# Reading back the inverse transforms of the first 512 tokens: a scratch of their own for the last group's rows, a later place in TensorE's list, and scratch rows of 2 KB

## The chip, the core and the metric

The kernel runs on one core of a Trainium2 chip. The core has a TensorE for matrix products (PE, with weight loads listed apart as PEld), VectorE (DVE), ScalarE (ACT), GpSimd (POOL), and SyncE (SP), which issues most DMA transfers. Each engine works through a list of its own; a semaphore holds an instruction until what it reads is there. The engines have on-chip memory (SBUF) of 128 partitions, and TensorE writes its sums to PSUM. DRAM is reached by DMA alone. DMA issues stand in the lists of SP, ScalarE and GpSimd, so what an issuing engine waits for holds up its transfers, and an issue takes its turn among that engine's other work.

The metric is the device time in microseconds (us) of one execution; lower is better.

## The reference

One layer on 2048 tokens of width 640: a normalization with modulation, a long convolution by a state-space model, a second normalization, and a gated feed-forward stage of width 1728.

```python
K = jnp.einsum("dn,dnl,dn->dl", Cc, P, dB).real          # P = exp(dt*A*l), the convolution kernel
Kf = rfft2(pad(K)); Uf = rfft2(pad(up))
y = irfft2(Uf * Kf, s=(1, 2 * L))[..., :L] + u * Dskip
...
x = A_u
sa, ca, ga, sb, cb, gb = ...                             # from silu(c) @ w_mod
h = _layernorm(x) * (1 + ca) + sa
x = x + ga * conv(h)
h = _layernorm(x) * (1 + cb) + sb
x = x + gb * (silu(h @ w1) * (h @ w3)) @ w2
```

## The kernel before

**Stages.** The convolution of length 2048 is a Fourier transform in two steps, 32 (NA) by 64 (NB) points, as matrix products. The 640 channels are NDC = 5 chunks of 128 (DC). A front part normalizes and transforms the input; a loop over 40 steps, whose order of work is the hand-written list `ROUND`, makes the transform of the convolution kernel and runs the steps of the chunks; its last eight steps' worth of chunk work, the eight groups g = 0 to 7 of the last chunk, stand in a plain loop over `tk` behind it. Then follows the feed-forward stage, on 512 tokens (four tiles of 128) at a time.

**A group.** For each chunk, eight groups of four frequencies go through: `stage2` (the second step of both forward transforms: products of uk with the table s2, in PSUM as p; 8 products), `k_copy` (ScalarE copies half of p to kc), `products` and `sums` (VectorE: T, then Y), and `inverse1` (8 products of Y with the table i1 into pz). s2 and i1 come by SP, in three buffers each. `z_store` copies pz (to zt, or in the last chunk to a tile of the pool h) and stores it in the DRAM scratch zs. For chunks 0 to 3 SP stores every second group (512 KB); for the last chunk `z_last` stores each group (256 KB) from ScalarE's queue.

**The second inverse step** needs, for a tile of 128 tokens, the rows of all 32 frequencies and both parts (64 rows) of 4 positions, so it reads zs across. The table for it is i2. A tile of such rows has the tag A in the profile, as the tiles of the exponentials before it had. In zs before, these rows lie as [chunk, position, part, frequency, channel], and a tile's load takes 4 pieces of 512 bytes for each of its 64 rows.

**The first 512 tokens** (tiles 0 to 3, `early`). The feed-forward stage begins with them, so their inverse is made beside the last groups. `x_part` takes chunks 0 to 3 from A (8 products, py) and VectorE adds the input xe into xm; `x_stats` are the statistics of the four chunks (st). ScalarE copies the fifth part of xe. The last chunk is taken apart. Groups 6 and 7 (from NG = 6) take the near way: `near_rows` makes their 16 rows straight from Y (8 products into a part of pz, and a copy to h), `near_cols` spreads them to the 512 tokens (pl<-h), with weights that `near_tables` makes on GpSimd; nothing goes through DRAM. Groups 0 to 5 take the far way: `z_last` stores them in zs, reads 24 frequencies of both parts back into the third part of A (two loads for each tile, those of tiles 0 to 2 on SP behind group 5's store, those of tile 3 on ScalarE behind group 6's), and `far_cols` adds 4 products for each tile (pl<-A; 64 rows, of which the unused ones are set to zero by memsets). VectorE then adds pl into xm, completes the statistics (mv), GpSimd and VectorE make the scales rs, `x_first` normalizes tiles 0 and 2 on ScalarE and 1 and 3 on VectorE (also called T in the profile), TensorE transposes them (ps<-ident,T) and `turn_a` makes xA, the operand of the feed-forward stage. Fillers (fill<-ident, ps<-idle) are products without use that keep TensorE's clock up.

**First weights.** `plain` computes the feed-forward blocks with weights split in a high and a low part (gh and gl for w1, uh and ul for w3): ScalarE casts the loaded rw, VectorE subtracts. Those of the first block, f = 0, are loaded behind the last i1 on SP.

**What sets the order.** A scheduler lists the instructions of each engine; `keep`, `ordered`, `acopy` and `keep_in_program_order` pin them to the order of the source, and `issue_after` puts a transfer behind a given instruction. In the loop over `tk`, i is the group whose `iv` and `zt` were just issued; this is where the work on the first 512 tokens is placed:

```python
if i == 3:
    x_stats(0)
if i in (2, 3, 5):
    x_part((0, 0, 0, 1, 0, 2)[i])
if i == 4:
    x_stats(1)
if i == 6:
    x_stats(2)
    near_cols(6)
```

`x_part(3)` stands in `near_rows` of group 7. In the trace, rows of py, pl and the near pz share L735, the line of the helper `ordered`; L148 is the helper of ScalarE's copies, and L111 that of `InOrder`, through which the feed-forward stage issues. The trace counts each of these fp32 products twice (x16 where the program has 8).

## Time and profile before

| | |
|---|---|
| runs (us) | 931.51, 931.76, 939.97; median 931.76 |
| the profiled execution (us) | 929.92 |
| its span in the profile (us) | 928.1 |
| granted TensorE clock, mean | 0.996 |
| busy: PE, PEld, DVE, ACT, POOL (us) | 890.6, 695.1, 698.6, 548.5, 259.1 |
| moved by DMA | 140.68 MB |

The busy time is a sum over the whole span and says little of a stage. The stretches of the span that the prediction shows give busy time, clock and transfers of a few microseconds each; the chain of waits goes back from the last instruction, at each step to what released it; the timelines give one engine's instructions in order, and in brackets how long the engine was idle before, and what ended it. "ACTq" and "SPq" are DMA issues on ScalarE's and SP's lists. Time in a timeline starts at the start of the span. A DMA group's last number is the median from issue to landing.

### The profile page before, as it was taken

To read this page: it belongs to the slowest core of one execution; us is meant where nothing else is said; L and a number is where in the kernel's file an instruction comes from. 1 tells how busy PE (TensorE), PEld (TensorE's weight loads), DVE (VectorE), ACT (ScalarE), POOL (GpSimd) and SP (SyncE) were. 2 spreads that over 40 slices of the span, in tenths; PEclk is the share of its full clock that TensorE was granted. 3 is DMA by queue.
4 is the path that set the end of the run, shared out by engine and by line. 5 is a ranking of instruction groups with operands and counts; after the bars stand their busy time and mean duration, and the time that the engine had idled before them with its cause. 6 is when DMAs were issued, how large, how long until landed. Compare 5 with 4: busy or idle time off the path is not lost.

```text
span 928.1 us, 21045 instructions
## 1 busy us (share of the span) xinstructions
PE 890.6 (96%) x8461; PEld 695.1 (75%) x8461; DVE 698.6 (75%) x1254; ACT 548.5 (59%) x811; POOL 259.1 (28%) x274
## 2 busy tenths in 40 slices
PE   5999889999999998999999999999999999999998
PEld 3766567777777666778888887778888888888886
DVE  6699888999999966877666655686876666664665
ACT  4899899999999742573433333566633333333432
POOL 3633454445446320231222201210522222200000
PEclk9999999999999999999999999999999999999999
DMA  8755897655656886942122117974222211103452
GB/s 257 238 207 201 265 230 216 177 160 156 177 160 173 205 258 217 249 180 86 57 85 85 46 49 211 260 257 154 89 71 72 85 58 57 58 28 100 146 179 101
DMA packets 103765, 140.68 MB, mean 152 GB/s; under 512 B 20212, under 2 KB 62964, under 8 KB 103668
## 3 DMA queue, kind: packets, MB, share of 16 engines
q1 hardware_dynamic: 100108, 129.48, 46.8%
q0 software_dynamic: 2048, 7.34, 2.4%
q10 hardware_dynamic: 1512, 2.52, 0.8%
q8 instruction: 66, 1.08, 0.5%
q14 instruction: 31, 0.25, 0.1%
HBM read 107.85 MB, written 31.46 MB: 150 GB/s over the span
## 4 chain that ended last, share of the span: by engine, by line
PE 69%; ACT 13%; DVE 11%; DMA 4%; issue 2%; SPq 0%; ACTq 0%; DVEq 0%; POOLq 0%; POOL 0%
PE ps L111 58%; PE p L676 3%; ACT A L145 2%; ACT ph L145 2%; DVE E L597 2%; PE pz L727 2%; ACT cs L145 2%; DVE uk L111 2%; PE pm L111 2%; ACT L145 2%; DVE A L604 1%; PE pt L637 1%; ACT kc L148 1%; DMA A<-zs 1%; DMA s<-in_s_dram 1%
## 5 line engine op out<-in xcount | busy, mean ns | idle before, releaser
L111 DVE TENSOR_TENSOR s<-ps,s 128x512 f32<-128x512 f32 x138 | 95.0, 689 | 79.9 <-PE ps L111 79.6
L111 DVE TENSOR_TENSOR gl<-rw,gh 128x640 fp32r<-128x640 f32 x87 | 77.9, 895 | 64.2 <-ACT gh L111 64.1
L570 POOL TENSOR_TENSOR ph<-thi,iota 128x1024 int32<-128x1024 int32 x40 | 85.9, 2149 | 141.9 <-DVE A L608 94.9
L111 ACT CAST gh<-rw 128x640 fp32r<-128x640 f32 x87 | 63.3, 727 | 102.8 <-PE ps L111 66.4
L111 POOL TENSOR_TENSOR S<-rw 128x256 f32<-128x256 f32 x46 | 35.4, 771 | 192.2 <-DVE S0l L111 167.9
L111 PE MATMUL ps<-xA,gh 128*128 128x512 f32 x280 | 88.4, 393 | 0.1
L111 PE MATMUL ps<-gh,uh 128*128 128x512 f32 x224 | 87.4, 390 | 0.0
L111 PE MATMUL ps<-gl,uh 128*128 128x512 f32 x224 | 87.2, 389 | 0.0
L676 PE MATMUL p<-uk,s 128*64 128x256 f32 x640 | 77.9, 385 | 7.2 <-DVE Y L701 2.4
L111 PE MATMUL ps<-gh,ul 128*128 128x512 f32 x208 | 81.1, 390 | 0.0
L676 PEld LDWEIGHTS p<-uk,s 128*64 128x64 f32 x640 | 44.6, 136 | 29.9 <-DVE Y L701 3.5
L111 PEld LDWEIGHTS ps<-xA,gh 128*128 128x128 f32 x280 | 52.2, 188 | 13.6 <-issue 1.0
L111 PE MATMUL ps<-xA,gl 128*128 128x512 f32 x140 | 54.5, 390 | 0.0
L604 DVE TENSOR_TENSOR A<-A,ph 128x1024 f32<-128x1024 f32 x40 | 51.9, 1297 | 0.0
L111 ACT ACTIVATE s<-ps 128x512 f32<-128x512 f32 (+1 forms) x33 | 19.6, 595 | 53.1 <-PE ps L111 53.1
L597 DVE TENSOR_TENSOR E<-A,cs 128x1024 f32<-128x1024 f32 x40 | 50.2, 1256 | 0.6 <-ACT A L145 0.6
L111 PEld LDWEIGHTS ps<-gl,uh 128*128 128x128 f32 x224 | 42.1, 188 | 9.0
L111 PEld LDWEIGHTS ps<-gh,uh 128*128 128x128 f32 x224 | 42.0, 188 | 8.8
L727 PE MATMUL pz<-Y,i 64*128 64x128 f32 x640 | 45.3, 282 | 0.7 <-ACT h L148 0.4
L111 PEld LDWEIGHTS ps<-gh,ul 128*128 128x128 f32 x208 | 39.0, 188 | 8.3
L574 POOL TENSOR_TENSOR ph<-ph,phi 128x512 int32<-128x512 int32 x40 | 44.5, 1114 | 2.5
L727 PEld LDWEIGHTS pz<-Y,i 64*128 64x128 f32 x640 | 39.7, 191 | 7.2 <-issue 5.9
(251 smaller groups left out, 2287.7 us busy)
## 6 DMA issues: line engine op xcount, KB each, us to landing
rw<-in_w_dram SPq DMA_DIRECT2D x52, 320.0 KB, 3.0
us<-u SPq DMA_DIRECT2D x16, 640.0 KB, 3.2
s<-in_s_dram SPq DMA_DIRECT2D x40, 256.0 KB, 5.1
i<-in_i_dram SPq DMA_DIRECT2D x40, 256.0 KB, 3.3
rw<-in_wg_dram SPq DMA_DIRECT2D x31, 320.0 KB, 3.3
rw<-in_wu_dram SPq DMA_DIRECT2D x28, 320.0 KB, 2.9
uk<-us SPq DMA_DIRECT2D x32, 256.0 KB, 4.6
zs<-zt SPq DMA_DIRECT2D x16, 512.0 KB, 4.5
```

The source lines that it names most:

```text
L111: ins = fn(*args, **kw)
L145: return tc.keep_in_program_order(S.activation(*args, **kw))
L148: return tc.keep_in_program_order(S.copy(out, in_))
L570: keep(G.tensor_tensor(p, bc(thi[:, s * SD:s * SD + SD], 2, NPH), bc(iota, 1, SD), op=OP.mult))
L574: keep(G.tensor_tensor(p[:, :, :NA], p[:, :, :NA], bc(phi[:, s * SD:s * SD + SD], 2, NA), op=OP.add))
L597: keep(V.tensor_tensor(EC[s][:, :, 1:3, :], AA[s][:, :, 1:3, :], mid(cs[s]), op=OP.mult))
L604: keep(V.tensor_tensor(A[:, :, 1:3, :], A[:, :, 1:3, :], mid(ph[s]), op=OP.mult))
L637: keep(PE.matmul(pt[c * 64:c * 64 + 64, g, :], kk[:, g, :], s1[:, c, :], start=True, stop=True, tile_position=(0, c * 64)))
L676: keep(PE.matmul(p2[par * 64:par * 64 + 64, pi, c, :], s2[:, pi * 2 + par, c * 64:c * 64 + 64], uk[:, 0:kn + 1:kn, f, :], start=True, stop ...
L727: ins = keep(PE.matmul(pz[:, par, (g % 2) * 2 + pi, :], i1[r, pi, c, :], Y[r, pi, c, :], start=(c == 0), stop=(c == 1), tile_position=(par ...
```

## The change

**Scratch layout.** zs becomes [chunk, frequency, part, position, channel]; a tile's load is then 64 rows of 2 KB, and a store writes 512 bytes at a time. The rows of i1, i2 and of the tiles A follow. **Last group.** Group 5's rows for the four tiles (positions 0 to 15) are also stored by two transfers of ScalarE in the new scratch ze, ahead of the group's whole store. SP loads the rows of groups 0 to 4 (40) for each tile from zs behind group 4's store, and the 8 rows of group 5 from ze behind the stores of group 5; ScalarE loads nothing. `far_cols` uses 48 rows, and the memsets are gone. **Later inverses.** `x_part` of tiles 0, 1, 2 stands at i = 4, 5, 6. **First weights.** Their loads stand ahead of the last i1 on SP. ScalarE's casts (`first_high`, into tiles of the pool rw) stand at i = 6 and in `near_rows` of group 7, VectorE's subtractions (`first_low`, in two parts, into tiles of the pool h) at the end of i = 6 and behind `x_first`. **Smaller.** The near rows take their part of i1 from the table i2d, which grows from 80 to 336 columns; two kinds of VectorE's instructions in `x_first` are pinned.

```diff
-    i2 = np.concatenate([np.cos(ang).T, -np.sin(ang).T] * 2)
+    i2 = np.concatenate([np.stack([np.cos(ang).T, -np.sin(ang).T], axis=1).reshape(2 * NA, NA)] * 2)
...
-    i1 = i1.reshape(*i1.shape[:-1], 2, NB).swapaxes(-1, -2).reshape(i1.shape)
+    i1d = i1[:, -4:].reshape(P, 4, 2, 2, NB)[..., :16].swapaxes(-1, -2)
...
-                i2d[fl, :, c, i * NA:i * NA + NA] = i2[c * NA + (6 + i) * 4 + fl]
+                i2d[fl, :, c, i * NA:i * NA + NA] = i2[2 * ((6 + i) * 4 + fl) + c]
             i2d[fl, :, c, 2 * NA:] = np.eye(16)
-    i2d = i2d.reshape(P, 2 * NA + 16)
+    i2d = np.concatenate([i2d.reshape(P, 2 * NA + 16), i1d.reshape(P, 8 * NA)], axis=1)
...
-    zs = dram.tile([NDC, NB, 2, NA, DC], F32, name="zs")
+    zs = dram.tile([NDC, NA, 2, NB, DC], F32, name="zs")
+    ze = dram.tile([4, 2, 16, DC], F32, name="ze")
...
-            near_rows(g, i1, Y, pz[:, 0, 2 - 2 * (g % 2), :])
+            near_rows(g, Y, pz[:, 0, 2 - 2 * (g % 2), :])
...
-    near = {}
...
+    near, first_w = {}, []
+
+    def first_high(i):
+        if i == 0:
+            near["raw"] = [xp.tile([P, KD, P], F32, name="rw", bufs=5) for _ in range(2)]
+            for w, name in zip(near["raw"], ("wg", "wu")):
+                with tc.issue_after(i1_last[0].ins):
+                    w_get(w, 0, name)
+            near["lo4"] = h_tile(F32R)
+        hi = xp.tile([P, KD, P], F32R, name="rw", bufs=5)
+        acopy(hi, near["raw"][i])
+        lo = h_tile(F32R).rearrange("p (k c) -> p k c", k=4)
+        first_w.append((near["raw"][i], hi, lo, near["lo4"][:, i * P:i * P + P]))
+
+    def first_low(w, hi, lo, lo4):
+        for out, k in ((lo, slice(4)), (lo4, 4)):
+            tc.keep_in_program_order(V.tensor_tensor(out, w[:, k], hi[:, k].bitcast(F32), op=OP.subtract))
 
...
 
     def near_tables():
 
-        hc = h_tile()[:, :2 * NA + 16]
...
+            G.tensor_tensor(w.rearrange("p (b a) -> p b a", b=16), bc(hc[:, 2 * NA:2 * NA + 16], 2, NA),
                             bc(hc[:, i * NA:i * NA + NA], 1, 16), op=OP.mult)
         near["z"] = h_tile()
-        for x, z, st in early:
...
             for c in range(2):
                 for par in range(2):
                     r, fl = slice(par * 64, par * 64 + 64), pi * 2 + par
...
             x_part(3)
+            first_high(1)
             near_cols(7)
             far_cols()
...
+    far = slice(64, 64 + 8 * NG)
+
     def far_cols():
...
-                ordered(near["pl"][b * NA:b * NA + NA, j * P:j * P + P], i2[64:], z[64:, b, 2 * DC:], start=False, stop=True,
+                ordered(near["pl"][b * NA:b * NA + NA, j * P:j * P + P], i2[far], z[far, 2, b], start=False, stop=True,
...
-    zst = [zs[k].rearrange("b c f d -> (b c) f d") for k in range(NDC)]
-    zsv = zs.rearrange("k b c f d -> (c f) b k d")
+    zst = [zs[k].rearrange("f c b d -> (c b) f d") for k in range(NDC)]
+    zev = ze.rearrange("f c b d -> (f c) b d")
+    zsv = zs.rearrange("k f c b d -> k (f c) b d")
...
+        for c in range(2) if g == NG - 1 else ():
+            S.dma_start(ze[:, c].rearrange("f b d -> b f d"), zt[c * 64:c * 64 + 16])
         stored = S.dma_start(zst[NDC - 1][:, g * 4:g * 4 + 4], zt)
-        for j in (range(3), (3,), ())[g - NG + 1] if g >= NG - 1 else ():
+        for j in range(4) if NG - 2 <= g < NG else ():
+            r = slice(0, 8 * g + 8) if g < NG - 1 else slice(8 * g, 8 * g + 8)
             with tc.issue_after(stored.ins):
-                for c in range(2):
-                    r = slice(c * 32, c * 32 + 4 * NG)
-                    ins = (S if j == 3 else nc.sync).dma_start(
-                        early[j][1][64 + r.start:64 + r.stop, :, 2 * DC:], zsv[r, 4 * j:4 * j + 4, NDC - 1])
-                    if j < 3:
-                        zlast[0] = ins
-
+                zlast[0] = nc.sync.dma_start(early[j][1][64 + r.start:64 + r.stop, 2],
+                                             (zsv[NDC - 1, r] if g < NG - 1 else zev)[:, 4 * j:4 * j + 4])
...
-            q.dma_start(z[hh * 64:hh * 64 + 64, :, kk * DC:kk * DC + DC], zsv[:, 4 * j:4 * j + 4, k])
+            q.dma_start(z[hh * 64:hh * 64 + 64, kk], zsv[k, :, 4 * j:4 * j + 4])
...
+    def h_tile(dt=F32):
+        return xp.tile([P, 512], dt, name="h", bufs=18)
 
...
-        return z.rearrange("p k s b -> p (k s b)").rearrange("p (b d) -> p b d", b=4)
-
-    ZW = (2 * DC, 3 * DC)
+        return z.rearrange("p k s b -> p (k s b)").rearrange("p (k b d) -> p k b d", k=3, b=4)
+
+    ZK = (2, 3)
...
-                ordered(py[hh][c, :2 * DC], i2[r], z[r, b, :2 * DC], start=True, stop=True,
...
+                ordered(py[hh][c, :2 * DC], i2[r], z[r, :2, b], start=True, stop=True,
...
-            if i == 3:
-                x_stats(0)
-            if i in (2, 3, 5):
-                x_part((0, 0, 0, 1, 0, 2)[i])
-            if i == 4:
-                x_stats(1)
+            if i in (4, 5, 6):
+                x_part(i - 4)
+            if i in (5, 6):
+                x_stats(i - 5)
             if i == 6:
+                near_cols(6)
+                first_high(0)
                 x_stats(2)
-                near_cols(6)
+                first_low(*first_w[0])
...
-    for name in first_w:
-        first_w[name] = xp.tile([P, KD, P], F32, name="rw", bufs=5)
-        with tc.issue_after(i1_last[0].ins):
-            w_get(first_w[name], 0, name)
-
...
-            V.scalar_tensor_tensor(rs[:, 2, :], mv[:, 2 * pair:2 * pair + 2, 0], -1.0, rs[:, 1, :],
-                                   op0=OP.mult, op1=OP.mult)
+            tc.keep_in_program_order(V.scalar_tensor_tensor(rs[:, 2, :], mv[:, 2 * pair:2 * pair + 2, 0], -1.0, rs[:, 1, :],
+                                                            op0=OP.mult, op1=OP.mult))
...
-                    V.tensor_scalar(xn, x, mv[:, j, 0:1], rs[:, 1, i:i + 1], op0=OP.subtract, op1=OP.mult)
+                    tc.keep_in_program_order(V.tensor_scalar(xn, x, mv[:, j, 0:1], rs[:, 1, i:i + 1],
+                                                             op0=OP.subtract, op1=OP.mult))
...
-                n = ZW[hh]
-                PE.matmul(py[hh][c, :n], i2[r], z[r, b, :n], start=True, stop=True, tile_position=(r.start, c.start))
+                n = ZK[hh] * DC
+                PE.matmul(py[hh][c, :n], i2[r], z[r, :ZK[hh], b], start=True, stop=True, tile_position=(r.start, c.start))
...
-    ahead = {(0, n): w for n, w in first_w.items()}
+    ahead = {}
...
+        if isinstance(w[0], list):
+            return w[0][k], w[1][k]
...
-        ws = first_plain.pop() if first_plain else plain_weights(simple[0], last_sum)
+        ws = first_plain.pop() if first_plain else [
+            ([hi[:, k] for k in range(KD)], [lo[:, k] for k in range(4)] + [lo4]) for _, hi, lo, lo4 in first_w]
...
             x_first(tiles, mv4)
+            first_low(*first_w[1])
```

On TensorE, around groups 2 to 6 of the last chunk (pz<-Y is `inverse1`, or with 32x128 `near_rows`; p is `stage2`; py is `x_part`), the list before:

```order
L727 MATMUL pz<-Y,i_5029 128x128 x8
L735 MATMUL py<-A,i_64 32x256 x8
L676 MATMUL p_5064<-uk,s_5062 64x256 x8
L727 MATMUL pz<-Y,i_5075 128x128 x8
L735 MATMUL py<-A,i_64 32x256 x8
L676 MATMUL p_5113<-uk,s_5111 64x256 x8
L727 MATMUL pz<-Y,i_5124 128x128 x8
L676 MATMUL p_5150<-uk,s_5148 64x256 x8
L727 MATMUL pz<-Y,i_5161 128x128 x8
L735 MATMUL py<-A,i_64 32x256 x8
L676 MATMUL p_5201<-uk,s_5199 64x256 x8
L735 MATMUL pz<-Y,i_5212 32x128 x8
```

and now:

```order
L728 MATMUL pz<-Y,i_5026 128x128 x8
L677 MATMUL p_5048<-uk,s_5046 64x256 x8
L728 MATMUL pz<-Y,i_5059 128x128 x8
L677 MATMUL p_5080<-uk,s_5078 64x256 x8
L728 MATMUL pz<-Y,i_5091 128x128 x8
L752 MATMUL py<-A,i_65 32x256 x8
L677 MATMUL p_5130<-uk,s_5128 64x256 x8
L728 MATMUL pz<-Y,i_5141 128x128 x8
L752 MATMUL py<-A,i_65 32x256 x8
L677 MATMUL p_5185<-uk,s_5183 64x256 x8
L752 MATMUL pz<-Y,h 32x128 x8
L728 MATMUL pz<-Y,i_5196 128x128 x8
```

The inverses of tiles 0 and 1 (py) have each moved behind two further pairs of p and pz, and that of tile 2 from ahead of the last p to behind the next pz.

On ScalarE, from the copy of group 6's pz (h<-pz 128x2x2x128) to the normalization (T), the list before:

```order
L148 COPY h<-pz 128x2x2x128
L798 DMA zs<-h 128x512
L803 DMA A<-zs 24x4x128 x2
L148 COPY h<-pz 128x128
L148 COPY xm<-xe_3784 128x128
L148 COPY h<-pz 128x2x2x128
L111 CAST gh<-rw 128x640
L798 DMA zs<-h 128x512
L111 CAST uh<-rw 128x640
L111 ACTIVATE T_5371<-xm,rs_5364 128x640
L111 ACTIVATE T_5376<-xm,rs_5367 128x640
```

and now (the casts into rw are those of the first weights):

```order
L149 COPY h<-pz 128x2x2x128
L820 DMA zs<-h 128x4x128
L149 COPY xm<-xe_3557 128x128
L149 CAST rw<-rw 128x640
L149 COPY h<-pz 128x128
L149 COPY xm<-xe_3785 128x128
L149 CAST rw<-rw 128x640
L149 COPY h<-pz 128x2x2x128
L111 ACTIVATE T_5371<-xm,rs_5364 128x640
L820 DMA zs<-h 128x4x128
L111 ACTIVATE T_5376<-xm,rs_5367 128x640
```

The two loads of A and the two casts no longer stand between the copies of group 7 and the first T, and the last store has moved behind that T.

On SP, from the i1 tables of the last groups to the first loads of the feed-forward stage, before:

```order
L711 DMA i_5212<-in_i_dram 128x512
L711 DMA i_5252<-in_i_dram 128x512
L830 DMA rw<-in_wg_dram 128x640
L830 DMA rw<-in_wu_dram 128x640
L803 DMA A<-zs 24x4x128 x6
L1089 DMA xm<-in_x_dram 128x640 x2
L111 DMA A<-zs 64x4x128 x8
```

and now:

```order
L712 DMA i_5196<-in_i_dram 128x512
L848 DMA rw<-in_wg_dram 128x640
L848 DMA rw<-in_wu_dram 128x640
L712 DMA i_5261<-in_i_dram 128x512
L824 DMA A<-zs 40x512 x4
L824 DMA A<-ze 8x512 x4
L1101 DMA xm<-in_x_dram 128x640 x2
L111 DMA A<-zs 64x512 x8
```

The weights have moved ahead of the last i1, and six loads of 24 rows in pieces of 512 bytes have become four of 40 and four of 8 rows of 2 KB, the latter from ze.

More of the change, by code (lines that the diff above doesn't have):

```diff
@@ L737, in near_tables @@
     def near_tables():
-        hc = h_tile()[:, :2 * NA + 16]
+        hc = h_tile()[:, :2 * NA + 16 + 8 * NA]
+        near["i1"] = hc[:, 2 * NA + 16:].rearrange("p (g c b) -> p g c b", g=4, c=2)
         nc.sync.dma_start(hc, a["i2d"])
@@ L742, in near_tables, with near_rows @@
             w = near["w", NG + i] = h_tile()
[L743 removed]
+            G.tensor_tensor(w.rearrange("p (b a) -> p b a", b=16), bc(hc[:, 2 * NA:2 * NA + 16], 2, NA),
                             bc(hc[:, i * NA:i * NA + NA], 1, 16), op=OP.mult)
         near["z"] = h_tile()
[L746 to L749 removed]
+    def near_rows(g, Y, pd):
         for pi in range(2):
@@ L754, in near_rows @@
                     r, fl = slice(par * 64, par * 64 + 64), pi * 2 + par
-                    ordered(pd[fl * 32:fl * 32 + 32], i1[r, pi, c, :32], Y[r, pi, c, :],
+                    ordered(pd[fl * 32:fl * 32 + 32], near["i1"][r, (g - NG) * 2 + pi, c], Y[r, pi, c, :],
                             start=(c == 0), stop=(c == 1), tile_position=(par * 64, fl * 32))
@@ L813, in z_load @@
             kk = k - 2 * hh
-            q.dma_start(z[hh * 64:hh * 64 + 64, :, kk * DC:kk * DC + DC], zsv[:, 4 * j:4 * j + 4, k])
+            q.dma_start(z[hh * 64:hh * 64 + 64, kk], zsv[k, :, 4 * j:4 * j + 4])
     def x_tile():
         return xp.tile([P, D], F32, name="xm", bufs=6)
-    def h_tile():
-        return xp.tile([P, 512], F32, name="h", bufs=18)
+    def h_tile(dt=F32):
+        return xp.tile([P, 512], dt, name="h", bufs=18)
     def z_tile():
         z = tz.tile([P, SD, 3, NA], F32, name="A")
-        return z.rearrange("p k s b -> p (k s b)").rearrange("p (b d) -> p b d", b=4)
-    ZW = (2 * DC, 3 * DC)
+        return z.rearrange("p k s b -> p (k s b)").rearrange("p (k b d) -> p k b d", k=3, b=4)
+    ZK = (2, 3)
     def w_get(w, f, name, q=nc.sync):
@@ L1011, in tile_kernel @@
     xp = None
-    first_w = dict.fromkeys(("wg", "wu"))
     ROUND = (
@@ L1134, in z_place @@
         return wq.tile([P, 2, 2, 512], F32, name=both).rearrange("p a b c -> p (a b c)")[:, :4 * 3 * DC].rearrange(
-            "p (b d) -> p b d", b=4)
+            "p (k b d) -> p k b d", k=3, b=4)
     def x_place(name):
@@ L1323, in plain @@
                         for i in range(1 if lo else 2):
-                            end = PE.matmul(ps, ws[i][:, k, :], x[k][lo], start=(k + i + lo == 0),
+                            end = PE.matmul(ps, wk(ws, k)[i], x[k][lo], start=(k + i + lo == 0),
                                             stop=(lo == 1 and k == KD - 1))
```

8 lines of the change are left out of this document (3 added, 5 removed).

## The prediction

> **What bounds the kernel now.** I read the page first, then busy time by stretches, the chain of waits, and last the timeline of each engine around the place that the change touches.
>
> ```profile
> span 928.1 us, 21045 instructions
> ...
> 345.00:351.00 6.00, 4.81 (x62) 2.97 (x62) 3.78 (x11) 1.96 (x4) 0.18 (x1) 1.00 0.90 281
> ...
> 367.00:368.00 1.00, 0.00 (x0) 0.00 (x0) 0.00 (x0) 0.00 (x0) 0.00 (x0) 0.90 0.80 260
> ...
> 374.00:375.00 1.00, 1.00 (x5) 0.83 (x4) 1.00 (x2) 0.82 (x2) 0.00 (x0) 0.68 0.54 169
> ...
> 400.00:450.00 50.00, 49.82 (x230) 40.99 (x229) 35.27 (x56) 25.99 (x47) 11.81 (x15) 1.00 0.32 106
> ```
>
> A row of stretches gives its length, then the busy time of TensorE (PE), of its weight loads, of VectorE (DVE), ScalarE (ACT) and GpSimd, the granted clock, and the DMA engines' share and GB/s. TensorE fills the feed-forward stage (49.82 of 50 us), so whatever brings its first product forward shortens the whole run by as much. Two gaps stand ahead of it: 1.2 us of idle PE in 345 to 351, and one that holds all of 367 to 368. In the second the clock falls (0.90 there, a mean over a stretch that ends at 0.50), and in 374 to 375 (0.68) it comes back. The chain of waits (start, length, what) goes through both:
>
> ```profile
> 342.72 4.93 DMA A<-zs
> ...
> 364.25 4.27 DMA A<-zs
> ...
> 369.30 2.01 PE pz L727 x16
> 371.31 1.58 PE fill L735 x6
> ...
> 376.62 2.12 ACT xA L111 x3
> ```
>
> The rows of the last chunk that tile 3 of the first 512 tokens needs land at 368.5; then come the last inverse product (pz), fillers, seven idle products and the transposes (both ps), and at 376.62 copies into the first operand xA of the feed-forward stage. All that the change can win lies in these 31 us.
>
> **The change, part by part.**
>
> *Inverses of the first tiles later (`x_part`, tag py).*
>
> ```profile
> 345.89 0.62 PE L735 MATMUL py<-A,i 64*32 64x256 f32 x2
> 347.70 0.66 PE L735 MATMUL py<-A,i 64*32 64x256 f32 x14 [1.19 <-DMA A<-zs]
> 348.29 1.95 PE L676 MATMUL p<-uk,s 128*64 128x256 f32 x16
> 350.16 1.16 PE L727 MATMUL pz<-Y,i 64*128 64x128 f32 x16
> 351.25 0.66 PE L735 MATMUL py<-A,i 64*32 64x256 f32 x16
> ```
>
> Two of sixteen py products issue at 345.89, the other fourteen at 347.70, when the load of 342.72 has landed. Sixteen take 348.29 - 347.70 = 0.59, so two take 0.08 and the wait is 347.70 - 345.97 = 1.7 us. In the new order two stages of p (1.87) and pz (1.09) come before them: TensorE gets there at 345.89 + 2 x 2.96 = 351.8, 4.2 us after today's landing. The wait goes: **-1.7**. No instruction is added; the py products of tiles 1 and 2 also move behind pz, which costs nothing in sum. On VectorE their sums move behind the products of the next group; what this does to its end is worked out below.
>
> *The far rows (`z_last`, `far_cols`).* Before, groups 0 to 5 are read back after group 5's store has landed, tile by tile, and tile 3 from ScalarE's queue behind group 6's store.
>
> ```profile
> 357.79 0.66 PE L735 MATMUL py<-A,i 64*32 64x256 f32 x16
> ...
> 360.25 0.65 PE L735 MATMUL pz<-Y,i 64*32 64x128 f32 x16
> ...
> 358.52 0.33 ACTq L798 DMA_DIRECT2D zs<-h  x1
> 361.31 2.41 SPq L803 DMA_DIRECT2D A<-zs  x6
> ...
> 363.66 0.89 ACTq L803 DMA_DIRECT2D A<-zs  x2
> ...
> 365.00 1.13 PE L735 MATMUL pl<-h 128*128 128x128 f32 x8 [0.42 <-ACT h L148]
> 366.06 0.86 PE L735 MATMUL pl<-A,i 64*32 64x128 f32 x24
> 368.65 0.65 PE L735 MATMUL pl<-A,i 64*32 64x128 f32 x8 [1.73 <-DMA A<-zs]
> ```
>
> Twenty-four far products start at 366.06 and are modelled to end at 366.92, the last of them 0.27 long: 0.6 us of issue. The other eight wait until 368.65, 2.0 us. They then take 0.58 at the low clock, against 0.2 at the rate of the 24. ScalarE issues two loads at 363.66 (0.89), which delays its copy of near rows and TensorE by 0.4. Both transfers leave ScalarE in the change. Gain if the new loads are in time: 2.0 + 0.2 (I keep half of the clock's 0.4) + 0.4 = **-2.6**.
>
> Are they in time? TensorE goes from group 5's pz to a py at 357.8 today; less 1.7 and less one py of 0.6, that is 355.5. Copy 0.6, then two stores of 32 KB to the scratch, then group 5's whole store. The loads of 8 rows follow on SP.
>
> ```profile
> DMA to landing us min/median/max: 2.5/3.6/5.5
> L803 SPq DMA_DIRECT2D A<-zs x6: 320/371/376, 361.3 to 363.3; - x6
> L111 SPq DMA_DIRECT2D A<-zs x30: 573/614/1377, 366.5 to 603.9; - x30
> ```
>
> The first row is the landing of the stores of h. The shape of three dimensions is not in the trace on ScalarE; on SP an issue takes 0.37 (small) or 0.61 (64x4x128), and I take 0.43 and 0.6. So the second scratch store issues at 356.6, lands at 359.1 to 360.2 (2.5 or 3.6 later; I take 2.8, what 358.52 to 361.31 shows), 359.4. Four loads at 0.37 end at 360.9; landing 2.5 later is 363.4. TensorE needs the last one after 24 far products: 369.30 - 4.3 - 0.2 = 364.8. Slack 1.4 us. At the upper ends (5.5 to land a store, and the 4.27 of the chain for a load) it would be 362.1 + 1.5 + 4.3 = 367.9, 3.1 too late. The 40-row loads hang on group 4's store, 3.6 us earlier, and have more room. On ScalarE, 2 x 0.43 + 0.6 of issues stand ahead of group 7's kc copy: 355.6 + 0.6 + 1.5 + 0.3 = 358.0, where TensorE's last p ends too (360.26 - 2.3): no wait, no slack either. The two weight loads go ahead of the last i1 load on SP; that load is needed 9 us after its issue.
>
> *VectorE up to there.* From its last kc at 358.0 + 0.6:
>
> ```profile
> 361.00 0.68 DVE L693 TENSOR_TENSOR T<-p,kc 128x512 f32<-128x512 f32 x1
> ...
> 364.68 0.76 DVE L857 TENSOR_TENSOR xm<-py,xe 128x256 f32<-128x256 f32 x2 [1.48 <-PE py L735]
> 365.36 0.86 DVE L863 BATCH_NORM_STATS2 st<-xm 128x6 f32<-128x128 f32 x4
> ...
> 373.88 0.82 DVE L111 TENSOR_TENSOR gl<-rw,gh 128x640 fp32r<-128x640 f32 x1
> ```
>
> Products and sums 2.2 (361.00 to 363.2), two tiles of xm 0.7 + 0.8 each, the low half of wg (0.82, and 0.1 because it is two instructions now): 358.65 + 2.2 + 3.0 + 0.9 = 364.8. TensorE is done with the far products at 365.0. So it does not bind, by 0.2 us; the low half of wg is hidden by that much and no more.
>
> *Casts of the first weights earlier.*
>
> ```profile
> 369.36 0.49 DVE L1075 TENSOR_TENSOR xm<-pl,xm 128x128 f32<-128x128 f32 x2 [3.14 <-PE pl L735]
> ...
> 373.28 0.16 DVE L111 SCALAR_TENSOR_TENSOR rs<-mv,rs 128x2 f32<-128x2 f32 x1 [0.58 <-POOL rs L111]
> ...
> 371.83 0.73 ACT L111 CAST gh<-rw 128x640 fp32r<-128x640 f32 x1
> ...
> 373.09 1.74 ACT L111 ACTIVATE T<-xm,rs 128x640 f32<-128x640 f32 x2
> ...
> 375.43 2.35 PE L111 MATMUL ps<-ident,T 128*128 128x128 f32 x20
> ```
>
> Before, two casts (of gh, 0.73, and of uh) stand from 371.83 to 373.09 between the statistics and ScalarE's normalization. From xm at 369.36 to xA at 376.62 are 7.3 us. After, ScalarE is free when rs of the second pair is there: 373.44 - 369.36 = 4.1, plus 0.92 for its tile (373.09 to 374.83 are two), plus two transposes and their latency, an estimate of 0.45 (two of twenty in 2.35 are 0.24, and about as much to release the copy): 5.5. TensorE's own list to that point takes 3.4 at full clock: pz 1.1, the fillers half of the chain's 1.58, and seven idle products at 0.22 (49.82 us for 230 in 400 to 450). Gain 7.3 - 5.5 = **-1.8**. VectorE's low half of wu (0.9) comes after the last T and before its first work on ps, 0.8 later: hidden, or 0.1.
>
> *Memset of four tiles gone, 2 KB rows, larger table.* GpSimd's memsets ended 15 us ahead of their use; 0. The 172 KB table load is used 20 us later; 0. Loads of z in the feed-forward stage are hidden by a full TensorE; 0.
>
> Sum: 1.7 + 2.6 + 1.8 = 6.1, of which I count 6.0: 928.1 - 6.0 = 922.1 of span. The profiled execution took 929.92, so 923.9; the median of the runs, 931.76, is 1.84 above it, which gives **925.8**.
>
> **The rivals.**
>
> *A, the scratch rows come late.* By the upper ends above, 3.1 us late; TensorE then has the gap of today and the clock falls as today. Of the three terms remain 1.7 and a part of the last: 931.76 - 1.7 = 930.1.
>
> *B, the clock.* PE idled from 366.9 to 368.65, and the clock stood at 0.50 for some 7 us, to its return in 374 to 375. In the new order TensorE has no gap as long, but one of 0.4 at the near copy, and about 0.8 between transposes while the last T is made. If these are enough, the half clock falls on the transposes and on the thirty first products (0.22 each): 7 us at half rate lose 3.4, giving 929.2. For it: a gap of 1.7 did it. Against it: the 1.2 of 346.5 did not. The Trainium skill, "TensorE: Matmul & The Clock Gate", section "HAM oscillation", asks for idle gaps above some 3.4 us. By that neither today's gap nor a new one costs anything; the trace does not agree, a gap of 1.7 sufficed here, and the measurement decides.
>
> *C, slower: stores in 512-byte rows.* Each partition's store was one run of 2 or 4 KB and is now 4 or 8 runs of 512 bytes, on the queue that also brings s2 and i1.
>
> ```profile
> 270.78 0.42 SPq L661 DMA_DIRECT2D s<-in_s_dram  x1
> ...
> s<-in_s_dram SPq DMA_DIRECT2D x40, 256.0 KB, 5.1
> uk<-us SPq DMA_DIRECT2D x32, 256.0 KB, 4.6
> zs<-zt SPq DMA_DIRECT2D x16, 512.0 KB, 4.5
> ...
> 284.63 1.73 PE L676 MATMUL p<-uk,s 128*64 128x256 f32 x14 [0.60 <-ACT uk L148]
> ```
>
> An s2 tile issued right behind a store at 270.78 is used three p later, 284.63: 13.9 us, with 5.1 to land, so 8.8 to spare. It decides only if a store takes 8.8 longer, from 4.5 to 13.3. 256 KB read in 512-byte rows (uk) take 4.6, so a store of 512 KB may take 9. Were it to go wrong by 1 us at each of sixteen stores, 925.8 + 16 = 942. The Trainium skill, "DMA: Bandwidth & Descriptors", section "Specifications", puts full rate at rows from 512 bytes up; by it the stores cost what they did.
>
> *D, no change:* ScalarE's three issues or a late i1 hold its kc copy, and the wait moves there; each us there is one of all. 1.5 us would leave 927.3, inside the range.
>
> **How the numbers follow.** My forecast 0.58 (with D; 923.5 to 928); A 0.15; B 0.12; C 0.07; and 0.08 that the stage gains more than these rows show. The range 922.5 to 930.5 holds the first, B and most of A: about 0.8. Within 1% is 922.4 to 941.1, about what a measurement here can tell from no change. The forecast, A and B lie inside it: same 0.85, faster 0.08, slower 0.07.
>
> **What would show it.** Right: no wait of py on a DMA, far products in one run of 32 without a wait, granted clock 1.00 between 360 and 375, T on ScalarE before the store of group 7, xA about 6 us earlier (370.5), and a stage behind it that is as full as now. Wrong: pl waiting for ze, 0.50 in any row of the transposes, p waiting for s2 in the loop, kc of the last group waiting for ScalarE's queue.

## The result

The changed kernel takes 924.12 us (median of 9 runs, 922.4 to 926.25). The kernel before took 930.11 us in the nine runs beside them; the three shown above were among these. The ratio is 0.9935, with a 95% interval of 0.9913 to 0.9956: 6.0 us faster, as much as the sum had counted, and a change of less than 1%. The forecast of 925.8 us stood on a median of three runs that was 1.65 us higher. The ratios here and below leave out four executions that ran slower than the rest: one of the kernel before (942.56 us) and one each of e2_cast_back, e3_no_ze and e7_layout_sp (1742 to 4154 us).

The profiled execution of the changed kernel took 925.65 us. First the page, and the stretches in which the kernel before stood idle or at half clock (columns as above):

```profile
span 923.9 us, 21042 instructions
...
363.00:369.00 6.00, 5.93 (x108) 4.79 (x101) 5.58 (x24) 2.61 (x7) 0.12 (x1) 1.00 0.64 197
367.00:368.00 1.00, 1.00 (x30) 0.80 (x23) 0.58 (x4) 0.00 (x0) 0.00 (x0) 1.00 0.71 272
...
374.00:375.00 1.00, 1.00 (x7) 0.79 (x6) 1.00 (x3) 1.00 (x3) 0.00 (x0) 1.00 0.69 123
```

TensorE is busy, and the clock is 1.00 throughout. In its timeline the last chunk, from its first p to the first product with xA (`ps<-xA,rw`), reads:

```profile
335.86 1.95 PE L677 MATMUL p<-uk,s 128*64 128x256 f32 x16
...
353.68 0.66 PE L752 MATMUL py<-A,i 64*32 64x256 f32 x16
...
359.71 0.65 PE L752 MATMUL pz<-Y,h 64*32 64x128 f32 x16
361.45 1.16 PE L728 MATMUL pz<-Y,i 64*128 64x128 f32 x16 [1.08 <-ACT h L149]
...
366.43 1.08 PE L752 MATMUL pl<-A,i 48*32 48x128 f32 x32
367.44 1.16 PE L728 MATMUL pz<-Y,i 64*128 64x128 f32 x16
368.53 0.94 PE L752 MATMUL fill<-ident 128*128 128x128 f32 x6
...
373.52 0.48 PE L111 MATMUL ps<-xA,rw 128*128 128x512 f32 x1
```

py comes without a wait, the 32 far products in one run, pz at its full rate. One wait is longer than before: 1.08 us ahead of group 6's pz, where it had been 0.41. The same marks of the kernel before:

```profile
334.01 1.95 PE L676 MATMUL p<-uk,s 128*64 128x256 f32 x16
...
369.23 2.08 PE L727 MATMUL pz<-Y,i 64*128 64x128 f32 x16
...
377.54 0.49 PE L111 MATMUL ps<-xA,gh 128*128 128x512 f32 x1
```

The last chunk starts at 334.01 before and at 335.86 in this execution, and between 333.6 and 335.0 in the ten other profiles below. So the point at which it starts differs from execution to execution by more than a part of this change is worth, and stretches inside the last chunk are compared instead. The **tail**, from the first p to the first product with xA, is 377.54 - 334.01 = 43.53 us before and 373.52 - 335.86 = 37.66 after: 5.87 less. Its **end piece**, from the pz behind the far rows, is 377.54 - 369.23 = 8.31 before and 373.52 - 367.44 = 6.08 after.

What held group 6's pz is on ScalarE:

```profile
351.44 0.38 ACTq L820 DMA_DIRECT2D zs<-h  x1
...
357.36 0.59 ACT L149 COPY h<-pz 128x512 f32<-128x512 f32 x1 [0.51 <-PE pz L728]
359.11 0.81 ACTq L819 DMA_DIRECT2D ze<-h  x2
359.96 0.44 ACTq L820 DMA_DIRECT2D zs<-h  x1
...
360.65 0.58 ACT L149 COPY kc<-p 128x512 f32<-128x512 f32 x1
```

The rows for the small scratch are ready at 357.95, but their store is issued at 359.11. The chain of waits tells what it waited for:

```profile
351.44 7.59 DMA zs<-h
359.07 0.04 issue
359.11 1.30 DMA ze<-h
```

That is the store of group 3 (351.44), whose data the new store does not touch: by the semaphores in the trace the transfers of SP and ScalarE take eight of them in turn, and the first small store has that of the transfer eight places ahead of it. The copy kc behind it on ScalarE came 0.8 us late, and the near rows' copy after it.

### The profile page after: what moved, and what is told of

It is laid out like the page before. It is cut to its first block, busy times and chain, and to the rows that moved or that the text cites. A ratio compares the mean times of both kernels' runs of the same rounds, so it can differ in the third digit from the quotient of the medians.

```text
span 923.9 us, 21042 instructions
## 1 busy us (share of the span) xinstructions
PE 887.7 (96%) x8461; PEld 693.4 (75%) x8461; DVE 698.9 (76%) x1256; ACT 549.1 (59%) x811; POOL 255.7 (28%) x270
## 3 DMA queue, kind: packets, MB, share of 16 engines
q8 instruction: 66, 1.08, 0.5%
## 4 chain that ended last, share of the span: by engine, by line
PE 70%; ACT 14%; DVE 11%; DMA 2%; issue 2%; DVEq 0%; ACTq 0%
PE ps L111 59%; PE p L677 3%; ACT A L146 3%; ACT ph L146 2%; ACT cs L146 2%; DVE E L598 2%; ACT L146 2%; DVE uk L111 2%; PE pm L111 2%; PE pz L728 1%; DVE A L605 1%; ACT kc L149 1%; PE pt L638 1%; DVE E L601 1%; ACT uk L149 1%
## 5 line engine op out<-in xcount | busy, mean ns | idle before, releaser
L111 POOL TENSOR_TENSOR S<-rw 128x256 f32<-128x256 f32 x46 | 35.2, 765 | 191.3 <-DVE S0l L111 166.7
L111 PE MATMUL ps<-xA,gh 128*128 128x512 f32 x270 | 84.0, 392 | 0.0
L111 PEld LDWEIGHTS ps<-xA,gh 128*128 128x128 f32 x270 | 50.2, 188 | 12.1 <-issue 1.0
L111 PE MATMUL ps<-xA,gl 128*128 128x512 f32 x135 | 52.6, 390 | 0.0
```

What stands on the lines that cost most here:

```text
L111: ins = fn(*args, **kw)
```

## The experiments

Ten profiles, three groups of runs, each with runs of the kernel before on the same chip (medians 931.18, 931.12 and 930.87 us). All times in us; "py wait" is from the end of py's first two products to the rest; e9_old_layout has no end piece, since part of its pz runs ahead of the last far products.

| run | what it is | time | ratio, 95% interval | py wait | end piece | tail |
|---|---|---|---|---|---|---|
| before | | 930.11 | 1 | 1.73 | 8.31 | 43.53 |
| after | the change | 924.12 | 0.9935 (0.9913-0.9956) | 0 | 6.08 | 37.66 |
| after_again | the change once more | 924.90 | 0.9928 (0.9904-0.9952) | 0 | 6.09 | 37.00 |
| e1_part_back | inverses early again | 926.65 | 0.9958 (0.9934-0.9982) | 2.1 | 6.09 | 40.08 |
| e2_cast_back | casts late again | 924.79 | 0.9941 (0.9910-0.9972) | 0 | 6.68 | 38.68 |
| e3_no_ze | without the small scratch | 923.83 | 0.9920 (0.9891-0.9949) | 0 | 6.09 | 36.98 |
| e4_layout_only | the layout alone | 928.32 | 0.9966 (0.9944-0.9987) | 2.0 | 7.41 | 42.15 |
| e5_before_fill | before, wait filled | 931.04 | 1.0004 (0.9983-1.0025) | 2.1 | 6.62 | 43.62 |
| e6_one_load | no small scratch, no split | 924.09 | 0.9917 (0.9894-0.9940) | 0 | 6.09 | 36.98 |
| e7_layout_sp | layout, tile 3 on SP | 929.68 | 0.9983 (0.9961-1.0005) | 3.4 | 6.67 | 42.68 |
| e8_py_between | e3 with py of tile 2 moved | 923.17 | 0.9918 (0.9899-0.9937) | 0 | 6.09 | 36.39 |
| e9_old_layout | e6 with the old layout | 924.94 | 0.9943 (0.9920-0.9965) | 0 | - | 37.54 |

### The inverses early again (e1_part_back)

```diff
-            if i in (4, 5, 6):
-                x_part(i - 4)
+            if i in (2, 3, 5):
+                x_part((0, 0, 0, 1, 0, 2)[i])
```

> The changed kernel with the inverses of tiles 0, 1 and 2 back at groups 2, 3 and 5 (statistics with them). Measure: the tail, from the last chunk's first p to the first product of the feed-forward stage, 43.5 us in the profile of before (334.01 to 377.54) and 37.7 in that of the changed kernel (335.86 to 373.52). My theory: py of tile 0 then waits again for its loads from zs; these were issued at 345.0 to 347.1 and TensorE would be there at 347.7, so with 3.8 to 5.8 us to land it waits 1.1 to 3.1 us: tail 39 to 41, and the run 1.5 to 3 us above the changed kernel. If the gap is above 2 us the clock may fall as after the gap of 1.7 before, which costs up to 3 more. Rival: with 2 KB rows the loads land early enough, or the wait is made up behind (the last group's rows come late anyway): tail 37.7 and no wait of py.

The wait is back, in this run's timeline of TensorE and its stretches:

```profile
346.90 0.62 PE L752 MATMUL py<-A,i 64*32 64x256 f32 x2
349.10 0.66 PE L752 MATMUL py<-A,i 64*32 64x256 f32 x14 [1.59 <-DMA A<-zs]
...
366.94 1.13 PE L752 MATMUL pl<-h 128*128 128x128 f32 x8 [0.95 <-ACT h L149]
...
345.00:351.00 6.00, 4.41 (x54) 2.49 (x50) 4.06 (x11) 1.47 (x3) 1.22 (x3) 1.00 0.98 264
```

It lasts 2.1 us, and the clock did not fall (1.00). The first term stands. The tail, 40.08, is inside what my theory gave, but not by the wait of py alone. Against the changed kernel's run without a hold on ScalarE (after_again, below: 37.00) it is 3.1 longer, and the other 0.95 is TensorE's wait for the copy of group 7's near rows, which stands on ScalarE behind the store of group 6 and a cast:

```profile
365.48 0.38 ACTq L820 DMA_DIRECT2D zs<-h  x1
365.91 0.72 ACT L149 CAST rw<-rw 128x640 fp32r<-128x640 f32 x1 [1.39 <-DMA A<-zs]
```

The store's rows are ready at 364.5; it is issued when a load of 40 rows, SP's, has landed (361.90 + 3.50), whose data it does not touch. It is the kind of hold seen above, at another place.

### The casts late again (e2_cast_back)

```diff
-            first_high(1)
...
+        for i in range(2) if pair == 0 else ():
+            first_high(i)
```

(`first_high(0)` leaves group 6 likewise, and both `first_low` stand behind `x_first`.)

> The changed kernel with ScalarE's casts of the first weights and VectorE's subtractions back in front of and behind the normalization (the weights' loads stay early). My theory: at full clock the chain from the statistics to xA is bound by ScalarE, so two casts (0.73 each) that stand ahead of the first T delay it by 1.1 to 1.2 us (in the changed kernel ScalarE is idle from 369.2 to 370.15, and T ends at 371.1): tail 38.8, run 1.1 us slower. Rival: TensorE's fillers and idle products, which end at 371.25, hide the casts and the third term of the prediction was the clock alone: tail within 0.3 of 37.7.

```profile
367.85 1.36 ACT L111 CAST rw<-rw 128x640 fp32r<-128x640 f32 x2 [0.44 <-ACT h L149]
369.11 1.74 ACT L111 ACTIVATE T<-xm,rs 128x640 f32<-128x640 f32 x2
...
367.75 1.86 PE L111 MATMUL ps<-idle 128*128 128x512 f32 x7
370.09 2.45 PE L111 MATMUL ps<-ident,T 128*128 128x128 f32 x20 [0.48 <-ACT T L111]
```

TensorE waits 0.48 us for T, and the end piece is 6.68 where it was 6.08: the casts are worth 0.6 us, between my theory (1.1) and the rival (0). The idle products cover the rest. That the tail, 38.68, comes near my theory's 38.8 is luck: the other 0.4 lies ahead of the end piece, where group 6's pz waited 1.50 us for the same reason as in the changed kernel. Here the store of group 3 took 7.93 us to land.

### Without the small scratch (e3_no_ze, e6_one_load), and the change once more

In e3_no_ze the two small stores are gone and the eight rows are read from zs behind group 5's whole store:

```diff
-        for c in range(2) if g == NG - 1 else ():
-            S.dma_start(ze[:, c].rearrange("f b d -> b f d"), zt[c * 64:c * 64 + 16])
...
-                                             (zsv[NDC - 1, r] if g < NG - 1 else zev)[:, 4 * j:4 * j + 4])
+                                             zsv[NDC - 1, r][:, 4 * j:4 * j + 4])
```

In e6_one_load the split is gone too:

```diff
-        for j in range(4) if NG - 2 <= g < NG else ():
-            r = slice(0, 8 * g + 8) if g < NG - 1 else slice(8 * g, 8 * g + 8)
+        for j in range(4) if g == NG - 1 else ():
             with tc.issue_after(stored.ins):
...
+                zlast[0] = nc.sync.dma_start(early[j][1][far, 2], zsv[NDC - 1, :8 * NG, 4 * j:4 * j + 4])
```

> The changed kernel without the small scratch: group 5's rows are read from the whole scratch, behind the group's whole store. In the changed kernel the two small stores wait on ScalarE until 359.07 for a store of group 3 that was issued at 351.44, and the copy kc behind them makes TensorE wait 1.08 us. My theory: the small scratch is what brings the rows in time; the whole store (256 KB) issued at about 359.1 lands 4 to 7.6 later, four loads behind it, so the last rows land at 366 to 370 where they are needed at 366.5: tail 38 to 41, and above 39.5 the clock falls too (2 more). Rival: its two issues on ScalarE (0.8 us) cost TensorE as much as the rows gain: tail 37.0 to 37.7, not slower.

> The changed kernel without the small scratch and without the split: all 48 rows of a tile in one load behind group 5's store, four loads on SP. Without the small scratch alone the tail was 36.98. My theory: the far rows have room by now, since SP is not held by ScalarE and the store of group 5 landed within 3 us: tail 36.9 to 37.4, pl without a wait or with one under 0.4. Rival: reading the first 40 rows early is what makes it: 48 rows in a load of 96 KB land 1 to 2 us later than the 8 rows, pl waits for tile 3, tail 38 to 39.5, with the clock at half behind it.

> The changed kernel once more, on the chip of the runs beside it, as their yardstick. Every theory: tail 37.3 to 38.1, 6 us below before.

My theory of e3_no_ze falls: its tail is 36.98, next to the rival's 37.0. The timelines of ScalarE, SP and TensorE in that run, and then of SP and TensorE in e6_one_load:

```profile
357.26 0.37 ACTq L816 DMA_DIRECT2D zs<-h  x1
...
358.54 2.81 SPq L820 DMA_DIRECT2D A<-zs  x8
...
364.71 1.08 PE L751 MATMUL pl<-A,i 48*32 48x128 f32 x32
```

```profile
359.69 1.73 SPq L819 DMA_DIRECT2D A<-zs  x4
...
364.83 1.08 PE L751 MATMUL pl<-A,i 48*32 48x128 f32 x32
```

All eight loads follow without a pause, since group 5's store landed 2.3 us after its issue, at 359.55, and the fifth load, the first that needs it, is issued at 360.08; the 32 products run without a wait. In e6_one_load four loads behind the same store are in time too, as my theory had it (tail 36.98). The changed kernel once more has a tail of 37.00, as both, 0.3 below what I had expected of it. There ScalarE issues the small stores at once, and pz waits as before:

```profile
356.84 1.27 ACTq L819 DMA_DIRECT2D ze<-h  x2
...
359.65 1.16 PE L728 MATMUL pz<-Y,i 64*128 64x128 f32 x16 [0.42 <-ACT h L149]
```

So the small scratch gains nothing here, and the 0.67 us more in the first profile (1.08 against 0.41) are the price of a store that took 7.59 us to land. That is no rare case. The first small store is ready 6.5 us behind the issue of group 3's store, whose semaphore it takes, and that store took 6.1 us in after_again, 6.8 in e3_no_ze, 7.4 in e6_one_load, 7.6 in after and 7.9 in e2_cast_back. Of the four profiles with the small scratch, three lost time on TensorE to a hold on ScalarE: 0.67 us (after), 1.09 (e2_cast_back) and 0.95 (e1_part_back). Without the pair of issues it is group 5's whole store that takes the semaphore in e3_no_ze; there ScalarE waited 0.36 us, kc was not late, and TensorE lost nothing.

### The layout alone, and ScalarE's queue (e4_layout_only, e7_layout_sp)

In e4_layout_only the other parts are undone; the last chunk's rows are read as before, in one load for each tile. e7_layout_sp differs from it in tile 3's load:

```diff
-        for j in (range(3), (3,), ())[g - NG + 1] if g >= NG - 1 else ():
+        for j in range(4) if g == NG - 1 else ():
             with tc.issue_after(stored.ins):
-                ins = (S if j == 3 else nc.sync).dma_start(early[j][1][far, 2], zsv[NDC - 1, :8 * NG, 4 * j:4 * j + 4])
-                if j < 3:
-                    zlast[0] = ins
+                zlast[0] = nc.sync.dma_start(early[j][1][far, 2], zsv[NDC - 1, :8 * NG, 4 * j:4 * j + 4])
```

> Only the layout of the scratch (and the table with the near rows' part) remains: inverses at groups 2, 3, 5, weights loaded and cast as before, the last chunk's rows read behind the stores of groups 5 and 6 as before, in one load for each tile. My theory: the layout alone is worth nothing: tail 43 to 44, py and pl wait as before, run within 1 us of before. Rival C: stores in rows of 512 bytes slow the loop, p waits for s2 and the run is 2 us or more slower than before. Third: loads in 2 KB rows land 1 us sooner and shorten both waits: tail 41 to 42.

> As the run with the layout alone (tail 42.15), but tile 3's rows too are loaded on SP behind group 5's store, and not on ScalarE behind group 6's. My theory: ScalarE's queue was what made tile 3 late: its load is issued at 364.3 on SP's clock of that run instead of landing at 368.7, the waits of 0.4 and 1.0 us before the last two tiles shrink to 0.4 or less, the clock stays at 1.00, and with the casts still in place the tail is 39.7 to 40.3. Rival: the loads are late wherever they are issued, since they all start behind group 5's store: waits of 1 us or more, half clock, tail 41.5 to 42.2.

TensorE and the clock in e4_layout_only:

```profile
366.26 0.64 PE L753 MATMUL pl<-A,i 48*32 48x128 f32 x16
367.28 0.42 PE L753 MATMUL pl<-A,i 48*32 48x128 f32 x8 [0.38 <-DMA A<-zs]
368.70 0.42 PE L753 MATMUL pl<-A,i 48*32 48x128 f32 x8 [0.99 <-DMA A<-zs]
369.05 1.16 PE L727 MATMUL pz<-Y,i 64*128 64x128 f32 x16
...
371.00:372.00 1.00, 0.90 (x4) 0.63 (x4) 0.72 (x5) 0.71 (x2) 0.84 (x3) 0.50 0.78 219
```

and TensorE in e7_layout_sp:

```profile
350.36 0.66 PE L753 MATMUL py<-A,i 64*32 64x256 f32 x14 [2.89 <-DMA A<-zs]
350.95 2.83 PE L676 MATMUL p<-uk,s 128*64 128x256 f32 x16
353.71 1.89 PE L727 MATMUL pz<-Y,i 64*128 64x128 f32 x16
...
369.98 1.08 PE L753 MATMUL pl<-A,i 48*32 48x128 f32 x32
```

With the layout alone both waits are there, and the clock falls as before, only later and for a shorter time. The tail, 42.15, is 1.4 us shorter than before, and the run 0.34% faster (interval 0.13 to 0.56%), so my theory (43 to 44, no gain) falls. Of the 1.4, 0.9 is the end piece, with less of it at half clock; the far rows give 0.4, and the near copy of group 7, which stands behind one load on ScalarE instead of two, 0.35, and the longer wait of py takes 0.25 back. Rival C is refuted: stores in rows of 512 bytes do not slow the loop (the ratio is below 1, and the last chunk starts at 334.3).

With tile 3 on SP the far products run as one: 1.01 us to the pz behind them, where e4_layout_only takes 2.79. The tail of e7_layout_sp missed my theory (39.7 to 40.3) and the rival's range, for another reason: its py waited 3.4 us, and the half clock behind that cost p 0.88 and pz 0.73. Less these, 42.68 - 3.43 - 1.61 = 37.6, which is the 37.0 of the changed kernel and the 0.6 of the casts; with a py wait of 2.0 it would be 39.6, next to the lower end of my theory.

Reading group 5 by way of the large scratch is thus not what made the rows late. That it was tile 3's place in ScalarE's queue is borne out but not shown alone, since the transfers were also quicker in e7_layout_sp: group 5's store took 3.5 us to land there against 4.1, and tile 2's load, on SP in both, 2.6 against 3.2. Nor was tile 3's load issued late on ScalarE: it went out 1.1 us after that store had landed, and on SP 1.3 after. What differs is its own landing, 4.4 us on ScalarE, where group 6's store of 256 KB was issued just ahead of it in the same queue, and 2.9 on SP. That the load had to follow this store is inferred. e9_old_layout, below, points the same way.

### The kernel before with its wait filled (e5_before_fill)

```diff
+            if j == 3:
+                near["fill"] = psS.tile([P, 2, 512], F32, name="fill", tag="B", bufs=1)
+                for _ in range(7):
+                    ordered(near["fill"][:, 0, :], idle[:, :P], idle, start=True, stop=True)
```

(in `far_cols`, ahead of tile 3's products.)

> The kernel before with seven idle products of 512 columns (1.7 us) in TensorE's wait for tile 3's far rows, and nothing else. My theory: the half clock after that wait cost as much as the casts did: with fillers the clock stays at 1.00, pz, fillers and idle products end 2.8 us earlier, and the second T on ScalarE (ends at 374.8, 0.4 earlier with pl) is what binds: f0 at about 376.0 where it was 377.54, tail 42.0. Rival: it was the casts alone, TensorE's clock did not matter, and only the last pl gets shorter: tail 43.1. Third: the clock falls in spite of the fillers: tail 43.5 to 44.

```profile
369.58 1.88 PE L735 MATMUL fill<-idle 128*128 128x512 f32 x7
371.39 0.42 PE L735 MATMUL pl<-A,i 64*32 64x128 f32 x8
371.75 1.16 PE L727 MATMUL pz<-Y,i 64*128 64x128 f32 x16
```

The clock is 1.00 to the end of the stage, and the end piece is 378.37 - 371.75 = 6.62 where the kernel before had 8.31, with the casts where they were: the half clock cost 1.7 us. The run is no faster (1.0004), and the tail (43.62) is what the third theory gave, but not for its reason: the last pl ends at 371.75, 37.0 us after the first p, where it was 35.2 before: part of that is the py wait (0.4 longer), the wait for the near copy (0.5 longer) and waits for the rows of tiles 1 and 2 (0.45 and 0.25); the rest is the fillers, behind which tile 3's products follow without a wait. When tile 3's rows landed this profile does not show. As a repair it fails; as a measure of the end piece it separates the clock from the casts.

### The old layout, and py in the gap (e9_old_layout, e8_py_between)

e9_old_layout is e6_one_load with zs, i1, i2 and the tiles as before, so with two loads for each tile:

```diff
-    zs = dram.tile([NDC, NA, 2, NB, DC], F32, name="zs")
+    zs = dram.tile([NDC, NB, 2, NA, DC], F32, name="zs")
...
+                for c in range(2):
+                    r = slice(c * 32, c * 32 + 4 * NG)
+                    zlast[0] = nc.sync.dma_start(early[j][1][64 + r.start:64 + r.stop, :, 2 * DC:],
+                                                 zsv[r, 4 * j:4 * j + 4, NDC - 1])
```

e8_py_between is e3_no_ze with the py of tile 2 between group 6's near rows and its pz:

```diff
+        if g == 6:
+            x_part(2, half=0)
         if g == 7:
             x_part(3)
```

(`half=0` is the TensorE part; VectorE's sum stays where it was, behind group 7's, which are pinned.)

> The run with one load for each tile (tail 36.98), but with the scratch laid out as before: stores in rows of 2 and 4 KB, loads in pieces of 512 bytes, so two loads of 24 rows for each of the four tiles, all eight on SP behind group 5's store, and the memsets are back. My theory: the layout was worth little by itself and what counts is SP's queue: eight issues of 0.37 take 3.0 us where four took 1.7, the last rows land 1 to 1.5 us later, pl waits 0 to 1.0 us: tail 37.0 to 38.0. Rival: rows of 2 KB are what brings the rows in time: pl waits 1.5 us or more and the clock falls: tail 39 to 41.

> The changed kernel without the small scratch (tail 36.98), and with the inverse of tile 2 (py) between group 6's near rows and its pz, where TensorE waits 0.41 us for ScalarE's copy of the near rows; VectorE's sums of group 7 stay ahead of tile 2's. My theory: py (0.59) covers the wait, all behind it comes 0.4 us earlier, VectorE has 0.5 us to spare ahead of the sum with pl: tail 36.5 to 36.65. Rival: VectorE or the copies for tile 2 bind at once, and the wait moves to the near rows of group 7 or to pl: tail 36.9 to 37.1.

In e9_old_layout the last tile's products start 0.4 us behind the others, with part of pz between them:

```profile
364.75 0.86 PE L752 MATMUL pl<-A,i 64*32 64x128 f32 x24
365.54 0.49 PE L728 MATMUL pz<-Y,i 64*128 64x128 f32 x4
365.96 0.42 PE L752 MATMUL pl<-A,i 64*32 64x128 f32 x8
```

So the 2 KB rows, with the one load for each tile that they allow, are worth 37.54 - 36.98 = 0.6 us here; my theory (37.0 to 38.0) holds and the rival does not. It also bears on the queue: in the old layout with all loads on SP the last tile is 0.4 us late, where the kernel before waited 2.0 for it, though this run differs from it in the order of py and in the casts as well. In e8_py_between TensorE no longer waits between the near rows and pz; py fills the place:

```profile
358.18 0.52 PE L755 MATMUL pz<-Y,h 64*32 64x128 f32 x10
...
358.64 0.62 PE L755 MATMUL py<-A,i 64*32 64x256 f32 x12
359.24 1.16 PE L731 MATMUL pz<-Y,i 64*128 64x128 f32 x16
```

The tail is 36.39, the shortest, 0.6 less than in e3_no_ze and 0.1 below what I expected. I had counted the wait of 0.41; but from the near rows to pz it is 1.06 us in both runs, 358.66 to 359.72 in e3_no_ze and 358.18 to 359.24 here, so all of py's 0.59 is gained. With 923.17 us its median is the lowest too, but its interval (0.9899 to 0.9937) overlaps that of the change, so only the profile tells them apart.

## Why the prediction was right, and where it was not

The time, the sign and the sum (6.0) were right. That they met so closely is in part luck: without the hold on ScalarE the tail is 6.5 shorter, and the hold took back in the first profile about what the last term had been counted too low. By its terms, the tail taken apart:

| term | predicted | measured |
|---|---|---|
| py | 1.7 | 1.73 |
| far rows and near copies | 2.6 | 2.5, less 0.67 in the first profile |
| casts and clock | 1.8 | 2.2: casts 0.6, clock 1.6 to 1.7 |
| sum | 6.1 | 6.5 in after_again, 5.87 in the first profile |

**py.** Right in place and size. Where py stands early, its wait is 1.7 to 3.4 us, by when the loads land, so the term is also the one with the largest spread.

**The far rows.** The 32 products take 1.01 us to the pz behind them (366.43 to 367.44) where they took 3.17 (366.06 to 369.23): 2.16, and the near copy of group 7 gives another 0.35. That is the size forecast. The prediction put the late rows of tile 3 down to ScalarE's load behind group 6's store; e7_layout_sp and e9_old_layout bear this out, but neither changes the queue alone with all else equal. What failed is the step about the small scratch: "the second scratch store issues at 356.6" took the issue to be free once the copy was done, and in the first profile even the first of the two was held by a store of an earlier group until 359.07, 1.16 us, as in e2_cast_back (1.5). And the step compared the small store's landing with no other way: that group 5's whole store would be in time as well (e3_no_ze, e6_one_load) was not worked out, though the landing of 2.8 us taken for the small store came from a whole one.

**The casts.** The step ("Gain 7.3 - 5.5", 1.8) was mis-sized, in sum by 0.4 and more in its parts. It read the 7.3 us from xm to xA as ScalarE's chain behind two casts; by e2_cast_back the casts are 0.6 of it and by e5_before_fill the half clock is 1.7. The prediction had the clock in view, with 0.2 for the pl products and as rival B, but gave the end of the stage to the casts.

**VectorE** was to have 0.2 us of room ahead of pl; it idled 0.42 there.

**The rivals.** A: the rows from the small scratch were in time even when their store was held for 1.2 us (357.95 to 359.11). B: the clock stayed at 1.00. C: refuted by e4_layout_only. D came true in part, for a reason the prediction did not name: an unrelated transfer's landing held ScalarE's queue, and with it kc for 0.67 us of TensorE's time in the first profile and 1.09 in e2_cast_back, and group 7's near copy for 0.95 in e1_part_back. In after_again nothing was held up.

Not settled: why the store of group 3 takes so long. It took 5.7 us (e8_py_between) to 7.9 in the six profiles with the later inverses that show its landing, and 3.5 and 3.2 in e4_layout_only and e7_layout_sp. In the six, two weight loads of 320 KB are issued beside it, in the two they come later; but there py's wait also lies ahead of the store, and no run moves the weight loads alone.

## What to carry to other kernels

Ask of a transfer on an engine that also computes what it waits for and what waits behind it: here such issues were held by the landing of transfers they had nothing to do with, and TensorE lost 0.67 to 1.09 us by it in three profiles. Before adding a faster path, ask whether the slow one is late: group 5's rows came in time by the large scratch, and the extra scratch gained nothing. When a wait is removed ahead of a stage, compare the stage behind it at both clocks before giving the gain to instructions moved there. Measure a change of half a per cent by a stretch between two fixed marks in the profile: three kernels with the same course agreed in the tail within 0.02 us, while whole executions of one kernel differed by 4. Look for holds in the stretch first: the two profiles of the changed kernel differ in it by 0.66.

## What the hardware showed beyond that

Equal gaps did not have equal results. In one profile, e4_layout_only, py's wait of 1.45 us by the profile, among the large products of p, left the clock at 1.00, while 0.38 and 0.99 us among the small products of pl brought it to 0.50. A wait of 2.89 us ahead of p did so too (e7_layout_sp), waits of 1.59 (e1_part_back) and 1.61 (e5_before_fill) did not. Nor do gaps among the small products bring it down each time: in e5_before_fill gaps of 0.89, 0.45 and 0.25 us stood among the products of pl within 3.5 us, and the clock stayed at 1.00. By stretches of half a microsecond the half clock lasted 3.4 us in e4_layout_only (370.4 to 373.8) and in e7_layout_sp (351.9 to 355.3), and 6.8 in the kernel before (367.8 to 374.6), twice as long. The Trainium skill, "TensorE: Matmul & The Clock Gate", section "HAM oscillation", speaks of windows of 3.4 us; the lengths agree, but not that it takes a gap of that length. What share of a window has to be busy, and whether small products count less, no run here tells apart.
